# One tile shape for the loop of a recurrent attention kernel, and four stream buffers instead of six

## The chip, the core and the metric

The kernel runs on one core of a Trainium2 chip. The metric is the device time of one execution in microseconds (us). Three runs of the kernel before took 1918.54, 1930.37 and 1937.62 us; their median is 1930.37 us. One further execution was recorded by the profiler and took 1924.12 us; all rows below are from it.

## The reference

Two attentions over the same 2048 x 640 input are mixed by a gate. All tensors are bfloat16.

```
g = sigmoid((x * gate_w).sum(-1))            # one gate per row
out = g * A(x) + (1 - g) * B(x)

A: mem = mem0                                # 8 rows of 640
   for s in range(64):                       # segments of 32 rows
       h = concat(mem, x[32 s : 32 s + 32])  # 40 rows
       q, k, v = h Wq, h Wk, h Wv            # 32 heads of 192 columns each
       p = softmax(q k^T * 192**-0.5, masked) # query i sees key j where i < 8 or i >= j
       o = (p v) Wo                          # 6144 -> 640
       mem = o[:8];  out_A[s] = o[8:]

B: 32 heads of 20 columns, each row attends to 8 rows spaced 2 apart; then one product by wo
```

A is a recurrence: the first eight output rows of a segment are the memory of the next one, so the 64 segments run one after the other.

## The kernel before, in words

The work runs in stages: B with the gate (`part_b`), a prepass that makes the products of the last 8 rows of every segment (`prepass`), the loop over the 64 segments (`part_a`), and an end that makes the outputs of those last rows for all segments (`part_z`). In the loop h holds 32 rows: 8 of memory and the first 24 of the segment; queries, keys and values of the other 8 rows come from the prepass through a DRAM buffer (`zpk_dram`) by `load_z` and `load_vz` (L494 to L498).

**Weights.** Wq, Wk, Wv and Wo are cut in 80 slices of 128 x 1536 (384 KB). Most stay in SBUF (tiles `wres` and `wlate`). N_STREAM of them, 15 here, are loaded again in each segment into WBUFS buffers, 6 here (tile `wst`, `load_slice`, L369 to L378). `weights_setup` (L335 to L367) spreads the streamed ones evenly over a modelled order of use: 163 ns for a slice and a table of gaps. SP's queue issues all these loads in the order of use, and each waits until the matmuls of the slice that held its buffer are done.

**The loop.** Heads are worked on in four groups R of eight, in two halves h of two groups. Each projection is four matmuls side by side: 32 rows of h stand in 32 columns of the array (`tile_position=(0, 32 * j)`), and each of the four column tiles multiplies its own 384 columns of a slice.

- `m_qk(i, kcs)` (L511): queries (i even) or keys (i odd) of group R = i // 2, in PSUM; when the last slice is done ScalarE copies 128 x 384 to SBUF (L524).
- `t_qk(i)` (L527): three transposes of 128 x 128 (L533), then VectorE copies all of it at once into `QTa` (L536) or `KT` (L540).
- `s_a(R, chunks)` (L549) and `s_b(h, chunks)` (L561): the scores of the own keys and of the prepass keys `KTz`. A head's 192 columns are one chunk of 128 and half of another. FULL chunks (t = 0, 2) use tiles of 128 rows x 32 columns; chunk t = 1 holds the halves of two heads, and HALF works on it in tiles of 64 x 32, rows 0 to 63 for one head and 64 to 127 for the other.
- `e_exp` (L571): exponential on ScalarE (L573), masks on VectorE. `e_norm` (L581): row sums by two matmuls with a 128 x 128 block matrix `bones` (L587, L589), Ln and Exp on ScalarE (L592, L593), two products on VectorE (L594, L595). Its PSUM buffer comes from the pool `psx` of two, which the transposes share.
- `m_v` (L597) values, `pv_half` (L610) probabilities times values in tiles of 32 rows x 128 or 64 columns (L622, L626), `o_group` (L652) the output product (L659).
- `sel` (L664): picks the 8 memory rows out of the output product by matmuls with `sel_m` (L669) in 128 x 128 tiles, three for part "oa" and two for "ob"; VectorE copies them into the next h (L672).

The order of TensorE and ScalarE is written out by hand (L507, and L675 to L734); VectorE and GpSimd are ordered by the framework. In a segment it is, shortened:

```
m_qk(0, 0-2) m_qk(1, 0) sel(ob) m_qk(1, 1-2) tail m_qk(0, 3-4) m_qk(1, 3-4)
m_qk(2, 0-2) t0 t1 m_qk(2, 3-4) m_qk(3) s_a(0)
m_qk(4, 0-3) t2 t3 m_qk(4, 4) [store, load_vz issued by ScalarE] m_qk(5) s_a(1) s_b(0) e_exp(0)
m_qk(6, 0-3) t4 t5 m_qk(6, 4) m_qk(7) e_norm(0) s_a(2) m_v(0) t6 t7 m_v(1) s_a(3) s_b(1) e_exp(1)
m_v(2) pv_half(0) e_norm(1) m_v(3) oa(0-5) pv_half(1) ob(0-2) oa(6-11) ob(3-8) sel(oa) ob(9-11)
```

Here t0 stands for `t_qk(0)`, oa and ob for `o_group`. `KT` is the first 768 columns of the tile `KV`, whose columns are used again in the same segment for the values `V` and the transposed outputs; `KTz`, `QTa`, the probabilities and the copied output product share the tile `ZQ`.

Of the kernel before, what the change touches and what calls it, by code (L numbers as in the profile page):

```python
# [10 lines left out]
BF = mybir.dt.bfloat16  # L11
F32 = mybir.dt.float32
I32 = mybir.dt.int32

N_STREAM = 15
N_LATE = 55
N_LATE2 = 11
WBUFS = 6

_DEV = {"mode": "full"}  # L20

# [3 lines left out]
class _K:  # L25
# [309 lines left out]
    def weights_setup(self):  # L335
# [125 lines left out]
    def part_a(self):  # L461
        nc, tc, KC, S = self.nc, self.tc, self.KC, self.S
# [3 lines left out]
        with ctx:  # L466
            pers = ctx.enter_context(tc.tile_pool(name="a_pers", bufs=1))
# [3 lines left out]
            KTz = ZQ[:, 608:992].rearrange("p (r c) -> p r c", c=12)  # L471
            Vz = ZQ[:, 224:608]
            QTa = ZQ[:, 992:2144].rearrange("p (b r c i) -> p b r c i", b=6, r=2, i=8)
            Es = [ZQ[:, 608 * h:608 * h + 224].rearrange("p (a f) -> p a f", a=2) for h in range(2)]
            zst = ZQ[:, 32:416]
            oTz = zst.rearrange("p (c q) -> p c q", q=8)
            whi = ZQ[:, 1376:1376 + 640]
            KV = pers.tile([128, 1536], BF, name="KV")
            KT = KV[:, 0:768].rearrange("p (c k) -> p c k", k=32)
            V = [KV[:, f0:f0 + 384] for f0 in (0, 768, 384, 1152)]  # L480
# [12 lines left out]

            def load_z(s):  # L494
                nc.scalar.dma_start(ZQ[:, 608:1376], self.zpk_dram[s, :, 384:1152])

            def load_vz(s):
                nc.scalar.dma_start(Vz, self.zpk_dram[s, :, 0:384])  # L498
# [9 lines left out]
            for s in range(nseg):  # L508
                pqs, sts, pSs = {}, {}, {}

                def m_qk(i, kcs):  # L511
                    R, m = i // 2, ("q", "k")[i % 2]
                    if i not in pqs:
                        pqs[i] = psm.tile([128, 512], F32, tag="m", name="ps_qk")
                    pq = pqs[i]
                    for kc in kcs:
                        sl = self.get_slice((m, R, kc))
                        for j in range(4):
                            nc.tensor.matmul(pq[32 * j:32 * j + 32, 0:384], lhsT=hT[:, kc, :],  # L519
                                             rhs=sl[:, 384 * j:384 * j + 384], start=(kc == 0), stop=(kc == KC - 1),  # L520
                                             tile_position=(0, 32 * j), skip_group_check=True)
                    if kcs[-1] == KC - 1:
                        st = KV[:, 768 + 384 * (i % 2):1152 + 384 * (i % 2)]
                        nc.scalar.copy(st, pq[:, 0:384])  # L524
                        sts[i] = st

                def t_qk(i):  # L527
                    R = i // 2
                    st = sts.pop(i)
                    pT = psx.tile([128, 1024], BF, tag="x", name="ps_qkT")  # L530
                    pT = pT[:, 0:384].rearrange("p (t j b i) -> p t j b i", t=3, j=4, i=8)
                    for t in range(3):
                        nc.tensor.transpose(pT[:, t, :, :, :].rearrange("p j b i -> p (j b i)"),  # L533
                                            st[:, 128 * t:128 * t + 128], self.ident[:])
                    if i % 2 == 0:
                        nc.vector.tensor_copy(  # L536
                            q_blocks(R)[:, 1:5, :, :].rearrange("p b c i -> p c b i"),
                            pT.rearrange("p t j b i -> p (t j) b i"))
                    else:
                        nc.vector.tensor_copy(KV[:, 384 * (R % 2):384 * (R % 2) + 384],  # L540
                                              pT.rearrange("p t j b i -> p (t j b i)"))

                def q_blocks(R):
                    b0 = 1 - R // 2
                    return QTa[:, b0:b0 + 5, R % 2, :, :]

                FULL, HALF = ((0, 0, 0, 128), (2, 1, 0, 128)), ((1, 0, 0, 64), (1, 1, 64, 128))

                def s_a(R, chunks):  # L549
# [3 lines left out]
                    for t, par, k0, k1 in chunks:  # L553
                        for j in range(4):
                            c = 4 * t + j
                            nc.tensor.matmul(pSs[h][32 * j:32 * j + 32, par, 40 * r:40 * r + 40],  # L556
                                             lhsT=KT[k0:k1, 12 * r + c, :], rhs=q_blocks(R)[k0:k1, :, c, :],
                                             start=(r == 0 and t != 1), stop=False,
                                             tile_position=(k0, 32 * j), skip_group_check=True)

                def s_b(h, chunks):  # L561
                    for t, par, k0, k1 in chunks:
                        for j in range(4):
                            c = 4 * t + j
                            nc.tensor.matmul(  # L565
                                pSs[h][32 * j:32 * j + 32, par, 80:112],
                                lhsT=KTz[k0:k1, :, c],
                                rhs=QTa[k0:k1, 1 - h:3 - h, :, c, :].rearrange("p b r i -> p r b i"),
                                start=False, stop=(t == 1), tile_position=(k0, 32 * j), skip_group_check=True)

                def e_exp(h):  # L571
                    E = Es[h]
# [8 lines left out]
                def e_norm(h):  # L581
                    E = Es[h]
                    EA = E[:, :, 0:80].rearrange("p a (r q) -> p a r q", q=40)
                    EB = E[:, :, 80:112].rearrange("p a (r q) -> p a r q", q=16)
                    pz = psx.tile([128, 512], F32, tag="x", name="ps_Z")
                    pz = pz[:, 0:160].rearrange("p (a r q) -> p a r q", a=2, r=2)
                    nc.tensor.matmul(pz.rearrange("p a r q -> p a (r q)"), lhsT=self.bones[:], rhs=E[:, :, 0:80],  # L587
                                     start=True, stop=False, skip_group_check=True)
                    nc.tensor.matmul(pz[:, :, :, 0:16], lhsT=self.bones[:], rhs=EB, start=False, stop=True,  # L589
                                     skip_group_check=True)  # L590
                    rz = pz
                    nc.scalar.activation(rz, pz, ACT.Ln)  # L592
# [92 lines left out]
                m_qk(3, range(KC)); s_a(0, FULL); s_a(0, HALF)  # L685
# [5 lines left out]
                for chunks in (FULL, HALF):  # L691
                    s_a(1, chunks)
                    s_b(0, chunks)
                e_exp(0)
                m_qk(6, (0, 1, 2, 3)); t_qk(4); t_qk(5); m_qk(6, (4,))
                m_qk(7, range(KC)); e_norm(0); s_a(2, FULL); s_a(2, HALF)
                m_v(0); t_qk(6); t_qk(7)
                m_v(1)
                for chunks in (FULL, HALF):
                    s_a(3, chunks)  # L700
                    s_b(1, chunks)
# [26 lines left out]
                if s + 1 < nseg:  # L728
                    pm = psS.tile([128, 2, 512], F32, tag="S", name="ps_mem")
# [136 lines left out]
```

## Time and profile before

| what | value |
|---|---|
| three runs, median | 1930.37 us |
| profiled execution, its time | 1924.12 us |
| its span, first to last instruction | 1922.4 us |
| mean granted TensorE clock | 0.987 |
| B and gate, prepass | 0 to about 240 us, to about 455 us |
| loop, 64 segments | about 460 to 1865 us |
| one segment, mean of 62 | 22.0 us (20.7 to 24.1) |
| end (`part_z`) | about 1865 to 1922 us |
| PE busy in the window 1000 to 1200 us | 187.04 us |
| DMA share and rate in that window | 0.90, 296 GB/s |

A segment is measured from one copy of "ob" (L734) to the next. In the profile PE stands for matmuls, PEld for weight loads, DVE for VectorE, ACT for ScalarE, POOL for GpSimd and SP for SyncE; a form such as 128*32 is the array tile, rows by columns, that a matmul uses. A row of a timeline gives the start, the length from the first start to the last end, the engine, the line, the tiles written and read, the count, and in brackets the idle time before it with what ended it. "issue" means that the engine waited for nothing that the profile shows.

### The profile page before, as it was taken

What the parts mean: (1) busy time and instruction counts of PE and PEld (TensorE: products, weight loads), DVE (VectorE), ACT (ScalarE), POOL (GpSimd) and SP (SyncE); (2) the same over time, 40 slices, a digit from 0 to 9 for tenths busy, and PEclk for the clock granted to TensorE, in tenths of its full rate; (3) what the DMA queues carried; (4) which work ended last, traced back from release to release, by engine and by line L of the source; (5) the groups of instructions that cost most, each with busy time, mean ns of one, the idle gap of its engine ahead of it and who ended that gap; (6) DMA issues with size and microseconds to landing.
All of it is one profiled execution on the core that took longest, in us unless ns stands there. A gap on an engine that the chain in (4) does not pass through costs nothing.

```text
span 1922.4 us, 90977 instructions
## 1 busy us (share of the span) xinstructions
PE 1731.9 (90%) x41120; PEld 1034.7 (54%) x41135; DVE 743.9 (39%) x2047; ACT 838.2 (44%) x1865; POOL 41.0 (2%) x70
## 2 busy tenths in 40 slices
PE   3898997897998999999999999999999999999989
PEld 1455543344555555555555555555555555555557
DVE  1565588922333333333333333333333333333320
ACT  1766688922333333443334433334433433333340
POOL 3111000001000000000000000000000000000000
PEclk9999999998999999999999999999999999999989
DMA  9112189869988899999999988899899988998981
GB/s 277 33 43 46 42 242 286 112 165 301 301 288 294 273 297 286 298 303 300 299 294 304 295 295 293 283 297 304 292 302 297 300 295 289 296 305 291 300 285 28
DMA packets 340968, 486.86 MB, mean 253 GB/s; under 512 B 148964, under 2 KB 209892, under 8 KB 340580
## 3 DMA queue, kind: packets, MB, share of 16 engines
q1 hardware_dynamic: 198608, 419.28, 66.2%
q10 hardware_dynamic: 141972, 61.76, 13.9%
q8 instruction: 322, 5.28, 1.1%
q14 instruction: 66, 0.54, 0.1%
HBM read 446.61 MB, written 35.91 MB: 251 GB/s over the span
## 4 chain that ended last, share of the span: by engine, by line
PE 73%; DVE 7%; ACT 7%; DMA 6%; issue 5%; ACTq 1%; SPq 0%; DVEq 0%
PE ps_qk L519 24%; PE ps_v L602 12%; PE ps_wo L659 11%; PE ps_qkT L533 6%; DVE ZS L73 5%; PE ps_S L556 3%; PE ps_oT L622 3%; PE ps_z L799 3%; PE ps_bqk L219 2%; ACT bP L242 2%; PE ps_pre L422 2%; ACT KV L524 2%; DVE KV L632 1%; PE ps_S L565 1%; DMA zpk_dram<-ZS 1%
## 5 line engine op out<-in xcount | busy, mean ns | idle before, releaser
L524 ACT CAST KV<-ps_qk 128x384 bf16<-128x384 f32 x512 | 238.8, 479 | 414.2 <-PE ps_qk L519 358.9
L519 PEld LDWEIGHTS <-hT 128*32 128x32 bf16 x10240 | 237.7, 96 | 183.4 <-issue 64.5
L519 PE MATMUL ps_qk<-wlate_k,hT 128*32 128x384 bf16 x4352 | 247.9, 328 | 4.3 <-issue 4.3
L602 PE MATMUL ps_v<-wlate_v,hT 128*32 128x384 bf16 x4096 | 226.7, 329 | 5.2 <-issue 5.1
L659 PEld LDWEIGHTS <-KV 128*32 128x32 bf16 x6144 | 170.0, 96 | 101.1 <-DVE KV L632 27.3
L519 PE MATMUL ps_qk<-wres_q,hT 128*32 128x384 bf16 x2560 | 164.6, 331 | 28.9 <-ACT KV L524 20.9
L536 DVE COPY ZQ<-ps_qkT 128x384 bf16<-128x384 bf16 x256 | 91.2, 356 | 237.2 <-PE ps_qkT L533 237.1
L659 PE MATMUL ps_wo<-wlate_oa,KV 128*32 128x384 bf16 x2304 | 154.1, 330 | 11.6 <-issue 3.9
L519 PE MATMUL ps_qk<-wst,hT 128*32 128x384 bf16 x1792 | 153.8, 330 | 1.9 <-issue 1.5
L602 PEld LDWEIGHTS <-hT 128*32 128x32 bf16 x5120 | 114.1, 96 | 73.0 <-issue 15.1
L632 DVE CAST KV<-ps_oT 128x192 bf16<-128x192 f32 x256 | 79.9, 353 | 170.7 <-ACT KV L632 170.7
L659 PE MATMUL ps_wo<-wlate_ob,KV 128*32 128x256 bf16 x2688 | 133.5, 278 | 12.2 <-issue 11.9
L533 PE MATMUL ps_qkT<-ident,KV 128*128 128x128 bf16 x1536 | 141.6, 221 | 2.1 <-ACT KV L606 0.3
L533 PEld LDWEIGHTS <-KV 128*128 128x128 bf16 x1536 | 87.9, 98 | 93.8 <-issue 92.6
L71 ACT CAST ZS<-ps_pre 128x512 bf16<-128x512 f32 x48 | 123.9, 3051 | 13.3 <-DMA zpk_dram<-ZS 6.4
L73 DVE CAST ZS<-ps_pre 128x512 bf16<-128x512 f32 x48 | 123.3, 2963 | 11.9 <-DMA zpk_dram<-ZS 7.7
L659 PE MATMUL ps_wo<-wst,KV 128*32 128x384 bf16 (+1 forms) x1152 | 115.3, 312 | 3.6 <-issue 2.7
L632 ACT CAST KV<-ps_oT 128x192 bf16<-128x192 f32 x256 | 69.7, 325 | 108.5 <-PE ps_oT L626 105.8
L519 PE MATMUL ps_qk<-wlate_q,hT 128*32 128x384 bf16 x1536 | 108.3, 330 | 0.0
L672 DVE CAST hT<-ps_mem 128x24 bf16<-128x24 f32 x126 | 22.5, 179 | 214.1 <-PE ps_mem L669 214.1
L556 PE MATMUL ps_S<-ZQ,KV 128*32 128x40 bf16 (+1 forms) x4096 | 102.7, 186 | 0.7 <-DMA ZQ<-zpk_dram 0.4
L556 PEld LDWEIGHTS <-KV 128*32 128x32 bf16 (+1 forms) x4096 | 78.0, 93 | 37.4 <-issue 1.8
(128 smaller groups left out, 2304.8 us busy)
## 6 DMA issues: line engine op xcount, KB each, us to landing
wst<-in_A_Wq_dram SPq DMA_DIRECT2D x260, 384.0 KB
wst<-in_A_Wv_dram SPq DMA_DIRECT2D x260, 384.0 KB
wst<-wscr SPq DMA_DIRECT2D x256, 384.0 KB
wst<-in_A_Wk_dram SPq DMA_DIRECT2D x195, 384.0 KB
zpk_dram<-ZS ACTq DMA_DIRECT2D x8, 1536.0 KB
ZQ<-zpk_dram ACTq DMA_DIRECT2D x64, 192.0 KB
wlate_k<-in_A_Wk_dram SPq DMA_DIRECT2D x17, 384.0 KB
wlate_v<-in_A_Wv_dram SPq DMA_DIRECT2D x16, 384.0 KB
```

The costliest lines, as they stand in the source:

```text
L71: nc.scalar.copy(out, in_)
L73: nc.vector.tensor_copy(out, in_)
L519: nc.tensor.matmul(pq[32 * j:32 * j + 32, 0:384], lhsT=hT[:, kc, :], rhs=sl[:, 384 * j:384 * j + 384], start=(kc == 0), stop=(kc == KC - 1 ...
L524: nc.scalar.copy(st, pq[:, 0:384])
L533: nc.tensor.transpose(pT[:, t, :, :, :].rearrange("p j b i -> p (j b i)"), st[:, 128 * t:128 * t + 128], self.ident[:])
L536: nc.vector.tensor_copy(q_blocks(R)[:, 1:5, :, :].rearrange("p b c i -> p c b i"), pT.rearrange("p t j b i -> p (t j) b i"))
L556: nc.tensor.matmul(pSs[h][32 * j:32 * j + 32, par, 40 * r:40 * r + 40], lhsT=KT[k0:k1, 12 * r + c, :], rhs=q_blocks(R)[k0:k1, :, c, :], st ...
L602: nc.tensor.matmul(pv[32 * j:32 * j + 32, 0:384], lhsT=hT[:, kc, :], rhs=sl[:, 384 * j:384 * j + 384], start=(kc == 0), stop=(kc == KC - 1 ...
L622: nc.tensor.matmul(out[:, r, t, :], lhsT=V[2 * h + r][ks, f0:f1], rhs=E[ks, par, 40 * r:40 * r + 40], start=(r == 0 and t == 0), stop=Fals ...
L632: cp(oTxs[2 * h + j // 2][:, 6 * (j % 2):6 * (j % 2) + 6, :], pos[j // 2][:, j % 2, 0:240].rearrange("p (c q) -> p c q", q=40)[:, :, 8:40])
L659: nc.tensor.matmul(pso[part][32 * jj:32 * jj + 32, 0:n], lhsT=oTxs[2 * (R // 2) + j // 2][:, 6 * (j % 2) + 3 * (R % 2) + t, :], rhs=o_weig ...
L799: nc.tensor.matmul(ps[32 * q:32 * q + 32, 0:nf], lhsT=oz[n, q][:, 24 * (R // 2) + 6 * j + 3 * (R % 2) + t, :], rhs=wo[part, c // nc_][:, c ...
```

## The change

The loop's products are brought to one tile shape, 128 rows x 32 columns; only `pv_half` keeps its own. A transpose becomes four, one for each 32 columns of its source; each of the two row-sum matmuls becomes four; each selection matmul becomes four. For the scores, chunk t = 1 is no longer worked on in 64-row tiles: the key half of the other head is zero instead. `KT` keeps rows 0 to 63 of that chunk with zeros below (written by GpSimd in each segment), and a new tile `KP` holds rows 64 to 127 with zeros above, for own keys (`KTp`) and prepass keys (`KTzp`). VectorE's copy of the transposed keys becomes three copies, and `load_z` is followed by a copy and a memset on GpSimd. `s_a` and `s_b` do all four chunks in one call. One weight slice fewer is streamed, and the stream has four buffers instead of six. The pools of PSUM and the order of the calls stay.

```diff
-N_STREAM = 15
+N_STREAM = 14
-WBUFS = 6
+WBUFS = 4
...
+            KP = pers.tile([128, 384], BF, name="KP")
+            nc.gpsimd.memset(KP[0:64, :], 0.0)
+            KTp = [KP[:, 128 * r:128 * r + 128].rearrange("p (j k) -> p j k", k=32) for r in range(2)]
+            KTzp = KP[:, 256:384].rearrange("p (r j) -> p r j", j=4)
...
             def load_z(s):
                 nc.scalar.dma_start(ZQ[:, 608:1376], self.zpk_dram[s, :, 384:1152])
+                nc.gpsimd.tensor_copy(KTzp[64:128], KTz[64:128, :, 4:8])
+                nc.gpsimd.memset(KTz[64:128, :, 4:8], 0.0)
...
-                        nc.tensor.transpose(pT[:, t, :, :, :].rearrange("p j b i -> p (j b i)"),
-                                            st[:, 128 * t:128 * t + 128], self.ident[:])
+                        for f in range(4):
+                            fs = slice(32 * f, 32 * f + 32)
+                            nc.tensor.transpose(pT[fs, t, :, :, :].rearrange("p j b i -> p (j b i)"),
+                                                st[:, 128 * t + 32 * f:128 * t + 32 * f + 32], self.ident[:],
+                                                tile_position=(0, 32 * f))
...
-                        nc.vector.tensor_copy(KV[:, 384 * (R % 2):384 * (R % 2) + 384],
-                                              pT.rearrange("p t j b i -> p (t j b i)"))
+                        kt = KV[:, 384 * (R % 2):384 * (R % 2) + 384].rearrange("p (t f) -> p t f", t=3)
+                        kp = pT.rearrange("p t j b i -> p t (j b i)")
+                        nc.vector.tensor_copy(kt[:, 0:3:2, :], kp[:, 0:3:2, :])
+                        nc.vector.tensor_copy(kt[0:64, 1, :], kp[0:64, 1, :])
+                        if R < 2:
+                            nc.gpsimd.memset(kt[64:128, 1, :], 0.0)
+                        nc.vector.tensor_copy(KTp[R % 2][64:128].rearrange("p j k -> p (j k)"), kp[64:128, 1, :])
...
-                FULL, HALF = ((0, 0, 0, 128), (2, 1, 0, 128)), ((1, 0, 0, 64), (1, 1, 64, 128))
+                CHUNKS = ((0, 0), (2, 1), (1, 0), (1, 1))
...
-                                             lhsT=KT[k0:k1, 12 * r + c, :], rhs=q_blocks(R)[k0:k1, :, c, :],
-                                             start=(r == 0 and t != 1), stop=False,
-                                             tile_position=(k0, 32 * j), skip_group_check=True)
+                                             lhsT=KTp[r][:, j, :] if (t, par) == (1, 1) else KT[:, 12 * r + c, :],
+                                             rhs=q_blocks(R)[:, :, c, :], start=(r == 0 and t != 1), stop=False,
+                                             tile_position=(0, 32 * j), skip_group_check=True)
...
-                    nc.tensor.matmul(pz.rearrange("p a r q -> p a (r q)"), lhsT=self.bones[:], rhs=E[:, :, 0:80],
-                                     start=True, stop=False, skip_group_check=True)
-                    nc.tensor.matmul(pz[:, :, :, 0:16], lhsT=self.bones[:], rhs=EB, start=False, stop=True,
-                                     skip_group_check=True)
+                    for z in range(2):
+                        for j in range(4):
+                            js = slice(32 * j, 32 * j + 32)
+                            out, rhs = (pz[js, :, :, 0:16], EB) if z else (
+                                pz[js].rearrange("p a r q -> p a (r q)"), E[:, :, 0:80])
+                            nc.tensor.matmul(out, lhsT=self.bones[:, js], rhs=rhs, start=(z == 0), stop=(z == 1),
+                                             tile_position=(0, 32 * j), skip_group_check=True)
...
-                        nc.tensor.matmul(pm[:, p, 8 * (m - m0):8 * (m - m0) + 8], lhsT=whi[:, m * 128:(m + 1) * 128],
-                                         rhs=self.sel_m[:], start=(m == m0), stop=(m == m1 - 1),
-                                         skip_group_check=True)
+                        for f in range(4):
+                            nc.tensor.matmul(pm[32 * f:32 * f + 32, p, 8 * (m - m0):8 * (m - m0) + 8],
+                                             lhsT=whi[:, m * 128 + 32 * f:m * 128 + 32 * f + 32], rhs=self.sel_m[:],
+                                             start=(m == m0), stop=(m == m1 - 1), tile_position=(0, 32 * f),
+                                             skip_group_check=True)
```

More of the change, by code (lines that the diff above doesn't have):

```diff
@@ L545, in q_blocks, with s_a @@
                     return QTa[:, b0:b0 + 5, R % 2, :, :]
-                FULL, HALF = ((0, 0, 0, 128), (2, 1, 0, 128)), ((1, 0, 0, 64), (1, 1, 64, 128))
-                def s_a(R, chunks):
+                CHUNKS = ((0, 0), (2, 1), (1, 0), (1, 1))
+                def s_a(R):
                     h, r = R // 2, R % 2
@@ L552, in s_a @@
                         pSs[h] = psS.tile([128, 2, 512], F32, tag="S", name="ps_S")
-                    for t, par, k0, k1 in chunks:
+                    for t, par in CHUNKS:
                         for j in range(4):
@@ L556, in s_a, with s_b @@
                             nc.tensor.matmul(pSs[h][32 * j:32 * j + 32, par, 40 * r:40 * r + 40],
-                                             lhsT=KT[k0:k1, 12 * r + c, :], rhs=q_blocks(R)[k0:k1, :, c, :],
-                                             start=(r == 0 and t != 1), stop=False,
-                                             tile_position=(k0, 32 * j), skip_group_check=True)
-                def s_b(h, chunks):
-                    for t, par, k0, k1 in chunks:
+                                             lhsT=KTp[r][:, j, :] if (t, par) == (1, 1) else KT[:, 12 * r + c, :],
+                                             rhs=q_blocks(R)[:, :, c, :], start=(r == 0 and t != 1), stop=False,
+                                             tile_position=(0, 32 * j), skip_group_check=True)
+                def s_b(h):
+                    for t, par in CHUNKS:
                         for j in range(4):
@@ L566, in s_b @@
                                 pSs[h][32 * j:32 * j + 32, par, 80:112],
-                                lhsT=KTz[k0:k1, :, c],
-                                rhs=QTa[k0:k1, 1 - h:3 - h, :, c, :].rearrange("p b r i -> p r b i"),
-                                start=False, stop=(t == 1), tile_position=(k0, 32 * j), skip_group_check=True)
+                                lhsT=KTzp[:, :, j] if (t, par) == (1, 1) else KTz[:, :, c],
+                                rhs=QTa[:, 1 - h:3 - h, :, c, :].rearrange("p b r i -> p r b i"),
+                                start=False, stop=(t == 1), tile_position=(0, 32 * j), skip_group_check=True)
                 def e_exp(h):
@@ L684, in part_a @@
                 m_qk(2, (0, 1, 2)); t_qk(0); t_qk(1); m_qk(2, (3, 4))
-                m_qk(3, range(KC)); s_a(0, FULL); s_a(0, HALF)
+                m_qk(3, range(KC)); s_a(0)
                 m_qk(4, (0, 1, 2, 3)); t_qk(2); t_qk(3); m_qk(4, (4,))
@@ L690, in part_a @@
                 m_qk(5, range(KC))
-                for chunks in (FULL, HALF):
-                    s_a(1, chunks)
-                    s_b(0, chunks)
+                s_a(1)
+                s_b(0)
                 e_exp(0)
                 m_qk(6, (0, 1, 2, 3)); t_qk(4); t_qk(5); m_qk(6, (4,))
-                m_qk(7, range(KC)); e_norm(0); s_a(2, FULL); s_a(2, HALF)
+                m_qk(7, range(KC)); e_norm(0); s_a(2)
                 m_v(0); t_qk(6); t_qk(7)
                 m_v(1)
-                for chunks in (FULL, HALF):
-                    s_a(3, chunks)
-                    s_b(1, chunks)
+                s_a(3)
+                s_b(1)
                 e_exp(1)
```

## The prediction, as put on record before the result

> **What bounds the kernel now.** I read the page first, then a timeline of one segment on PE and ACT, then the waits of the steady loop (600 to 1800 us, 55 segments), then the DMA queues of that window. The page:
>
> ```profile
> PE 1731.9 (90%) x41120; PEld 1034.7 (54%) x41135; DVE 743.9 (39%) x2047; ACT 838.2 (44%) x1865; POOL 41.0 (2%) x70
> ...
> q8 instruction: 322, 5.28, 1.1%
> ...
> PE 73%; DVE 7%; ACT 7%; DMA 6%; issue 5%; ACTq 1%; SPq 0%; DVEq 0%
> ```
>
> TensorE's order of work is the chain, and busy 90% hides what is lost inside it. The timeline of PE shows the loss:
>
> ```profile
> 1003.89 0.67 PE L519 MATMUL ps_qk<-wres_q,hT 128*32 128x384 bf16 x12 [0.25 <-ACT KV L524]
> 1004.49 0.51 PE L533 MATMUL ps_qkT<-ident,KV 128*128 128x128 bf16 x6
> 1004.93 0.35 PE L519 MATMUL ps_qk<-wres_q,hT 128*32 128x384 bf16 x4
> 1005.11 0.34 PE L519 MATMUL ps_qk<-wst,hT 128*32 128x384 bf16 x4
> 1005.27 0.99 PE L519 MATMUL ps_qk<-wlate_k,hT 128*32 128x384 bf16 x20
> 1006.08 0.36 PE L556 MATMUL ps_S<-ZQ,KV 128*32 128x40 bf16 x16
> 1006.37 0.35 PE L519 MATMUL ps_qk<-wst,hT 128*32 128x384 bf16 x4
> ```
>
> Four projection matmuls side by side start every 0.163 us (1005.11 to 1005.27). The third group of the first row starts at 1004.22, so the transposes could start at 1004.38; they start at 1004.49. Six of them start 0.057 apart ((0.51 - 0.22) / 5), so the next group could start at 1004.83; it starts at 1004.93. Each change of tile shape costs about 0.10 us, and a segment has 29.
>
> The second loss is irregular. In the waits of PE, "issue" names no engine and no transfer, yet lasts up to 1.8 us; one such hole, in the timeline:
>
> ```profile
> PE ps_wo L659 <- issue: 16.9, 20, 1.8
> PE ps_qk L519 <- ACT KV L524: 14.1, 55, 0.3
> PE ps_oT L622 <- issue: 9.8, 13, 1.5
> PE ps_oT L626 <- issue: 9.2, 10, 1.4
> ```
> ```profile
> 1039.83 0.18 PE L626 MATMUL ps_oT<-ZQ 32*64 32x32 bf16 x2
> 1040.84 0.21 PE L626 MATMUL ps_oT<-ZQ 32*64 32x32 bf16 x6 [0.82 <-issue]
> ```
>
> Queue q8 explains it. Its 322 packets carry 5.28 MB, 16.4 KB each; PE and PEld have 82,255 instructions, 64 B each, 255 to a packet: q8 brings TensorE its own instructions in blocks of 256. The packet records around the hole: one runs from 1038.40 to 1039.54, and PE resumes 1.30 us after it. Over the loop, 74 holes of over 0.5 us lie 255.3 instructions (or a multiple) apart, and each ends 1.2 to 1.7 us (mean 1.41) after a q8 packet. After a hole the next packet starts 1.1 to 4.0 us (mean 2.23) later and takes 1.02: one block ahead, no more. A refill takes 2.23 + 1.02 + 1.41 = 4.66 us beside the stream, and a segment's 565 matmuls and as many weight loads are 4.41 blocks in 22.0 us. The mean hole by the block's own time (hole left out), from the starts in the records: 0.93 us for blocks under 3.5 us (29 of them), 0.61 for 3.5 to 4, 0.35 for 4 to 4.5, 0.13 for 4.5 to 5, 0.04 to 5.5, none above. That is 0.27 a block, 1.2 us a segment; a segment's own time is 20.8.
>
> SP's queue is not behind: a slice lands 3.84 us after its issue (median of the packet records; 4.5 at the 95th percentile, 5.3 at most), and no PE row above waits for one.
>
> **What the change saves on TensorE, per segment.** It removes 23 of the 29 changes of shape (the 6 of pv_half stay).
> - Transposes: four pairs, 0.11 before and 0.10 after each: 0.84. The 24 quarter transposes of a pair go four at a time, like the projections, at the old 0.057 a group: no more.
> - Scores: 16 matmuls took 0.29 with their two changes (1006.08 to 1006.37). Four groups of four take 0.03 each, since eight start within 0.06 in the next call: 0.12, saving 0.17, twice. The 32 of s_a and s_b go from 0.48 to 0.30 (prepass keys, read with a stride, 0.045 a group): 0.175, twice. Together 0.69.
> - Sums: 0.19 around e_norm(0), 0.10 in e_norm(1). Selections: 0.10 and 0.07 for each part: 0.34.
>
> Gross 2.16 us. Some of it only uncovers another engine:
> - t7 waits for the PSUM buffer of e_norm(0). From the last group of m_qk(7) the chain is fixed: ACT's copy, Ln, Exp, DVE's products, 2.03 us (1011.07 to 1013.10). TensorE would come 1.36 after. It already waits 0.2; all saved in between is lost: sums 0.19, s_a(2) 0.17, one entry 0.10: 0.46.
> - t5 needs ACT's copy of keys, queued behind two DMA issues:
>
> ```profile
> 1008.03 0.48 ACT L524 CAST KV<-ps_qk 128x384 bf16<-128x384 f32 x1 [1.19 <-PE ps_qk L519]
> 1008.11 0.58 ACTq L752 DMA_DIRECT2D out_dram<-a  x1
> 1008.73 0.48 ACTq L498 DMA_DIRECT2D ZQ<-zpk_dram  x1
> 1009.31 0.48 ACT L524 CAST KV<-ps_qk 128x384 bf16<-128x384 f32 x1 [0.80 <-PE ps_S L565]
> ```
> The copy is ready 2.27 after the group m_qk(4, 4) starts; TensorE comes at 2.10 (5 + 4 groups 1.47, scores 0.30, t4 0.17, one step 0.16): 0.17 lost.
> - sel(oa) comes when ACT's copy L727 is done, as 45 waits of it already show: entry 0.10 lost. The first m_qk(0, 3-4) waits for DVE's L672: 0.03.
>
> Lost 0.76, net 1.40 us (between 1.2, if pv_half(1) stays on DVE's L594, and 2.16, if nothing is uncovered). The segment's own time falls from 20.8 to 19.4.
>
> **What it adds.** DVE: one key copy (351 ns) becomes three. By the rows 128x384 (351), 128x24 (183) and 128x16 (175) they end about 0.24 us later. The last is ready 0.94 us after the last transpose; five to seven groups (0.82 to 1.14) and three score groups (0.09) stand before its reader. Cost 0; without that cover at most 0.24 a group R. POOL: three memsets and a copy per segment, by 32-row rows 0.18 to 0.26 us each, bounded by 128x640 at 0.82. They stand behind load_z's landing, some 4 us after an issue that precedes sel(oa) by 2; s_a(0) comes 5 us after it: 0, or up to 1 us if a landing takes 6. The own load of one more resident slice at the start: 1.3 us (384 KB at 296 GB/s), taken as 1.
>
> Buffers: a slice now must land within four uses less its own, 4 x 19.4/14 - 0.6 = 4.9 us, against 3.84 (six: 6 x 22.0/15 - 0.6 = 8.2). Mostly covered: 0; the other end is 0.5 us on two slices a segment, 1 us. One slice of 15 less lowers the load of the DMA engines by 6% a segment.
>
> TensorE's instructions: transposes 24 to 96, sums 4 to 16, selections 5 to 20: 99 matmuls and 99 weight loads more, 664 pairs, 5.19 blocks in 19.4 us: 3.74 us of own time a block instead of 4.7. By the table above, a hole of 0.65 a block (0.61 at 3.75, and a little for the spread to both sides), 3.4 us a segment instead of 1.2. Bounds: 0.27 as now; 1.0 if each hole leaves the next block without the lead that it has now (refill 4.66 against 3.74, spread included). I take 0.65, which has rows of this very loop.
>
> **The sum.** 19.4 + 3.4 = 22.8 us against 22.0: +0.8, times 64 = 51 us, and 1 at the start. From the profiled 1924 us: 1976. (The median of runs is 1930, 0.3% above that execution.)
>
> [...]
>
> [...]
>
> **The rivals.**
> - Refills stay covered: faster. Place: the block boundaries; price: 0.27 a block as now, 19.4 + 1.4 = 20.8, 64 x -1.2 gives 1847. It decides below (22.0 - 19.4) / 5.19 = 0.50 us a block. For it: six per cent less stream, and q8 shares its engines with the stream. Against it: the 58 blocks under 4 us, with 0.77 on average.
> - Refills bind fully: 1.0 a block, 19.4 + 5.2 = 24.6, 1924 + 64 x 2.6 = 2090. For it: two holes in a row happen already; against it: a slower segment also thins the stream, and with it the 2.23 us of queueing.
> - Four buffers are too few: refills as now, but 1 us a segment of landing on top of the forecast: 2040. Against it: 1 us of slack at the median.
> - The changes of shape don't go away, since the stall is the operand's and not the shape's: net 0, refills at 20.8 / 5.19 = 4.0 us, 0.48 a block: 1924 + 64 x 1.3 = 2007. Against it: the same 0.10 at every change, and none between L556 and L565.
>
> **How the numbers follow.** Forecast (0.45 to 0.85 us a block, 1905 to 2040, its own likely stretch 1930 to 2010): 0.52, of which 0.10 lies within 1%. Refills covered (1800 to 1905): 0.24, of which 0.02 within 1%. Refills bind fully: 0.14; late landings: 0.05; shape stalls stay: 0.05. A measurement can tell about 1% (19 us) from no change. Faster 0.22, same 0.12, slower 0.66. The range 1860 to 2090 leaves out the lower end of the covered case and what lies above full binding.
>
> **What would show it.** Right: some 372 q8 packets (50 more); holes at every second boundary or more, 3 us a segment; no step at L533, L587, L669 beyond 0.163; t7 still 2.0 us behind m_qk(7). Wrong: "issue" no larger than now, or PE waiting for wst, POOL or the third key copy.

## The result

Four runs after: 2017.72 to 2034.44 us, median 2026.68; four before: median 1927.06. The ratio is 1.0505 [1.0466, 1.0545]: about 5% slower. The profiled execution took 2028.84 us (span 2027.0, mean granted clock 0.970). Line numbers move in the kernel after: ACT's key and query copy is L530, the transposes L541, `s_a` L570, `s_b` L579, the sums L606, `m_v` L619, `pv_half` L639 and L643, `o_group` L676, the selections L687.

From the page of the kernel after, the lines of busy time, of the queue q8, and of the chain that ended last:

```profile
PE 1680.0 (83%) x47456; PEld 1099.0 (54%) x47456; DVE 821.5 (41%) x2559; ACT 841.1 (41%) x1865; POOL 94.5 (5%) x327
...
q8 instruction: 371, 6.08, 1.2%
...
PE 58%; issue 12%; DVE 10%; ACT 9%; DMA 9%; ACTq 1%; SPq 0%; DVEq 0%; POOL 0%
```

PE has 6,300 matmuls more and is busy 52 us less, yet the span is longer: PE's share of the chain fell from 73% to 58%, "issue" rose from 5% to 12%. q8 has 49 packets more. The mean over the whole loop, before and then after (columns: window, its length, busy time and count of PE, PEld, DVE, ACT, POOL, then the granted clock, the DMA share, GB/s):

```profile
474.00:1860.00 1386.00, 1290.20 (x35481) 787.69 (x35477) 464.18 (x1698) 540.77 (x1507) 0.00 (x0) 1.00 0.91 296
```
```profile
478.00:1966.00 1488.00, 1230.96 (x41696) 848.47 (x41683) 541.11 (x2203) 543.50 (x1507) 51.49 (x248) 0.98 0.84 260
```

PE is busy 59 us less and the window is 102 us longer. The mean segment went from 21.99 to 23.63 us (62 of them); ahead of the loop there are 4 us more, and the end takes the same (57.1 and 56.5). The DMA share fell with the pace of the loop; nothing here says that the stream holds it back. PE's timeline after, at the place that the prediction showed of before (start, length, idle time before in brackets):

```profile
1045.35 0.67 PE L525 MATMUL ps_qk<-wres_q,hT 128*32 128x384 bf16 x12 [0.26 <-ACT KV L530]
1045.84 0.52 PE L541 MATMUL ps_qkT<-ident,KV 128*32 128x128 bf16 x24
1046.17 0.51 PE L525 MATMUL ps_qk<-wres_q,hT 128*32 128x384 bf16 x8
1046.49 0.35 PE L525 MATMUL ps_qk<-wst,hT 128*32 128x384 bf16 x4
1046.66 0.51 PE L525 MATMUL ps_qk<-wlate_k,hT 128*32 128x384 bf16 x6
1048.43 0.67 PE L525 MATMUL ps_qk<-wlate_k,hT 128*32 128x384 bf16 x10 [1.27 <-issue]
```

The transposes follow the third group by 0.16 us (1045.84 - 1045.35 - 2 x 0.163), and the next projection starts 0.33 us after them, six groups at 0.056: the steps at the changes of shape are gone. Then, in the middle of `m_qk(3)`, PE stands still for 1.27 us for nothing that the profile names; a q8 packet had run from 1046.16 to 1047.10, and PE resumes 1.33 us after its end. The waits of PE after (600 to 1900 us: what waited for what, us in total, times, longest):

```profile
PE ps_qk L525 <- issue: 33.5, 38, 1.9
PE ps_v L619 <- issue: 27.5, 26, 2.1
PE ps_qkT L541 <- issue: 26.7, 26, 2.0
PE ps_oT L639 <- issue: 21.7, 20, 2.1
PE ps_S L570 <- issue: 18.0, 22, 2.6
PE ps_qkT L541 <- DVE ZQ L612: 16.6, 32, 0.6
PE ps_qk L525 <- ACT KV L530: 13.6, 53, 0.3
PE ps_oT L639 <- DVE KV L625: 10.5, 29, 0.4
...
PE ps_qk L525 <- DMA wst<-in_A_Wk_dram: 1.7, 4, 0.6
PE ps_qk L525 <- DMA wst<-in_A_Wq_dram: 1.4, 3, 0.9
```

Holes now sit in every stage, the projections first. Counted as in the prediction (over 0.5 us, ended by an instruction that comes 1.1 to 1.75 us after a q8 packet), there are 186 of them against 76, 3.43 us a segment against 1.22. They keep to a place in the stream of instructions: counted with the sequencer's own, every 256th. Of the 197 gaps between starts over 0.3 us that end 1.2 to 1.6 us after a q8 packet, 190 fall on the same eight of the 256 places (before: 85 of 96). The waits for `wst` are short. Two rows are new: t7 behind DVE's L612, and `pv_half` behind L625, VectorE's copy of values.

### The profile page after: what moved, and what is told of

Same layout as the page of the kernel before. It is cut to its first block, busy times and chain, and to the rows that moved or that the text cites. A ratio compares the mean times of both kernels' runs of the same rounds, so it can differ in the third digit from the quotient of the medians.

```text
span 2027.0 us, 104719 instructions
## 1 busy us (share of the span) xinstructions
PE 1680.0 (83%) x47456; PEld 1099.0 (54%) x47456; DVE 821.5 (41%) x2559; ACT 841.1 (41%) x1865; POOL 94.5 (5%) x327
## 4 chain that ended last, share of the span: by engine, by line
PE 58%; issue 12%; DVE 10%; ACT 9%; DMA 9%; ACTq 1%; SPq 0%; DVEq 0%; POOL 0%
PE ps_qk L525 19%; PE ps_wo L676 8%; PE ps_v L619 8%; DVE ZS L73 5%; PE ps_qkT L541 4%; DMA wst<-in_A_Wq_dram 3%; PE ps_oT L639 3%; PE ps_z L816 3%; PE ps_pre L422 2%; ACT bP L242 2%; PE ps_bqk L219 2%; DVE KV L649 2%; PE ps_S L570 2%; ACT KV L649 2%; DMA wst<-in_A_Wk_dram 1%
## 5 line engine op out<-in xcount | busy, mean ns | idle before, releaser
L530 ACT CAST KV<-ps_qk 128x384 bf16<-128x384 f32 x512 | 239.0, 479 | 438.5 <-PE ps_qk L525 390.0
L525 PEld LDWEIGHTS <-hT 128*32 128x32 bf16 x10240 | 268.2, 96 | 208.2 <-issue 107.6
L525 PE MATMUL ps_qk<-wlate_k,hT 128*32 128x384 bf16 x4096 | 261.4, 329 | 21.2 <-issue 20.3
L619 PE MATMUL ps_v<-wlate_v,hT 128*32 128x384 bf16 x4096 | 255.8, 335 | 26.9 <-issue 26.9
L676 PEld LDWEIGHTS <-KV 128*32 128x32 bf16 x6144 | 179.5, 99 | 103.5 <-DVE KV L649 32.6
L541 PE MATMUL ps_qkT<-ident,KV 128*32 128x128 bf16 x6144 | 156.8, 221 | 49.8 <-issue 30.5
L525 PE MATMUL ps_qk<-wres_q,hT 128*32 128x384 bf16 x2816 | 177.1, 330 | 24.3 <-ACT KV L530 19.2
L619 PEld LDWEIGHTS <-hT 128*32 128x32 bf16 x5120 | 139.2, 98 | 80.4 <-issue 48.1
L541 PEld LDWEIGHTS <-KV 128*32 128x32 bf16 x6144 | 128.7, 98 | 82.7 <-issue 37.8
L676 PE MATMUL ps_wo<-wlate_oa,KV 128*32 128x384 bf16 x2560 | 157.8, 346 | 6.1 <-issue 4.5
L676 PE MATMUL ps_wo<-wlate_ob,KV 128*32 128x256 bf16 x2688 | 136.5, 284 | 3.6 <-issue 3.5
L525 PE MATMUL ps_qk<-wlate_q,hT 128*32 128x384 bf16 x1536 | 126.2, 328 | 7.5 <-issue 7.5
L676 PE MATMUL ps_wo<-wst,KV 128*32 128x384 bf16 (+1 forms) x896 | 105.2, 320 | 12.0 <-issue 2.2
L619 PE MATMUL ps_v<-wst,hT 128*32 128x384 bf16 x1024 | 100.4, 334 | 7.3 <-issue 7.2
L639 PE MATMUL ps_oT<-ZQ,KV 32*128 32x40 bf16 (+1 forms) x4096 | 77.0, 186 | 35.3 <-issue 21.7
L587 ACT ACTIVATE ZQ<-ps_S 128x224 bf16<-128x224 f32 x128 | 46.0, 360 | 132.7 <-PE ps_S L579 128.3
```

The source lines that it names most:

```text
L541: nc.tensor.transpose(pT[fs, t, :, :, :].rearrange("p j b i -> p (j b i)"), st[:, 128 * t + 32 * f:128 * t + 32 * f + 32], self.ident[:], ...
L587: nc.scalar.activation(E, pSs[h][:, :, 0:112], ACT.Exp, scale=scale_a)
L619: nc.tensor.matmul(pv[32 * j:32 * j + 32, 0:384], lhsT=hT[:, kc, :], rhs=sl[:, 384 * j:384 * j + 384], start=(kc == 0), stop=(kc == KC - 1 ...
L639: nc.tensor.matmul(out[:, r, t, :], lhsT=V[2 * h + r][ks, f0:f1], rhs=E[ks, par, 40 * r:40 * r + 40], start=(r == 0 and t == 0), stop=Fals ...
L676: nc.tensor.matmul(pso[part][32 * jj:32 * jj + 32, 0:n], lhsT=oTxs[2 * (R // 2) + j // 2][:, 6 * (j % 2) + 3 * (R % 2) + t, :], rhs=o_weig ...
```

## The experiments

The theory: TensorE's instructions come in blocks that are refilled one ahead, and more and shorter instructions leave the refill uncovered. The rivals: the thinner stream (late slices), the added VectorE and GpSimd work, or the 32-column loads themselves.

| kernel | median us | before, same chip | ratio [95%] | segment | holes | rest |
|---|---|---|---|---|---|---|
| b_stream | 1929.81 | 1932.31 | 0.9995 [0.9971, 1.0019] | 22.16 | 1.30 | 20.86 |
| b_trans | 2008.84 | 1932.31 | 1.0416 [1.0372, 1.0460] | 23.40 | 3.13 | 20.27 |
| b_splitv | 2056.45 | 1932.31 | 1.0661 [1.0610, 1.0712] | 24.23 | 2.53 | 21.70 |
| b_scores | 1928.31 | 1932.31 | 0.9987 [0.9959, 1.0015] | 22.18 | 1.53 | 20.65 |
| b_nostream | 1841.86 | 1932.52 | 0.9517 [0.9485, 0.9549] | 20.81 | 0.28 | 20.52 |
| a_nostream | 1828.31 | 1932.52 | 0.9442 [0.9406, 0.9478] | 20.58 | 0.86 | 19.71 |
| a_t128 | 1947.87 | 1932.52 | 1.0080 [1.0051, 1.0110] | 22.31 | 1.59 | 20.72 |
| b_scores5 | 1928.06 | 1932.52 | 0.9980 [0.9955, 1.0004] | 22.09 | 1.74 | 20.36 |
| s5_norm | 1916.26 | 1930.14 | 0.9909 [0.9876, 0.9941] | 21.75 | 1.55 | 20.20 |
| b_norm | 1923.43 | 1930.14 | 0.9968 [0.9942, 0.9995] | 22.01 | 1.38 | 20.63 |

Segment, holes and rest are us per segment from each profile; here holes count from 0.3 us, and the rest, the segment's own time, is the segment without them. On this scale before has 21.99 = 1.30 + 20.69 and after 23.63 = 3.58 + 20.04.

### b_stream: only the buffers and the streamed slices

Before, with
```diff
-N_STREAM = 15
+N_STREAM = 14
-WBUFS = 6
+WBUFS = 4
```


> The kernel before with only the stream's part of the change (14 streamed slices, four buffers). Theory (TensorE waits for the refills of its instruction blocks; 99 more matmuls and weight loads a segment made it slower): the 565 matmuls of a segment stay, so 4.41 blocks and holes of about 1.2 us a segment stay or shrink a little with 6% less stream; 1910 to 1932 us. Rival (four buffers let slices land late): most of the 100 us of the change, 1970 to 2030 us, with waits of PE for wst.

The same time, the same holes. From its waits of PE (600 to 1800 us):

```profile
PE ps_oT L622 <- issue: 13.1, 18, 1.8
...
PE ps_v L602 <- DMA wst<-in_A_Wv_dram: 1.4, 2, 1.1
```

In the whole loop 8 waits for a slice take 3.5 us. Four buffers instead of six and one slice less together change nothing that can be told; the run does not tell the two apart.

### b_trans: only the transposes

Before, with the transposes of the change:
```diff
-                        nc.tensor.transpose(pT[:, t, :, :, :].rearrange("p j b i -> p (j b i)"),
-                                            st[:, 128 * t:128 * t + 128], self.ident[:])
+                        for f in range(4):
+                            fs = slice(32 * f, 32 * f + 32)
+                            nc.tensor.transpose(pT[fs, t, :, :, :].rearrange("p j b i -> p (j b i)"),
+                                                st[:, 128 * t + 32 * f:128 * t + 32 * f + 32], self.ident[:],
+                                                tile_position=(0, 32 * f))
```


> The kernel before with only the transposes in four 32-column pieces, stream as before (15 slices, six buffers). Theory: 637 matmuls a segment, 4.98 blocks; the eight changes of shape go (0.84 us), own time a block about 4.0 us, holes about 0.45 a block, 2.2 us a segment instead of 1.2: about 22.3 us a segment, 1950 us (1925 to 1985). Rival (buffers or key copies made the change slow): the drains' 0.84 us come through, 1870 to 1890 us.

The direction was right and the size too small: 4.2% slower, most of the whole loss, with no added copy, GpSimd work or buffer change. Its waits of PE (600 to 1800 us):

```profile
PE ps_qk L519 <- issue: 28.2, 31, 2.3
PE ps_oT L625 <- issue: 24.1, 24, 2.2
PE ps_v L605 <- issue: 18.6, 20, 2.1
```

Few of the holes are at the transposes: they lie in the projections and `pv_half`, wherever a block ends. The segment's 72 pairs more (a pair is a load and its matmul) add 1.83 us of holes; own time fell by only 0.42. Part of the missing gain may be the clock: 54 us of the loop ran at half of it (see the last section), by accounting up to 0.35 us a segment.

### b_splitv: more instructions, same shape, same columns

Before, each `m_v` matmul of 384 columns as two of 192:
```diff
-                        for j in range(4):
-                            nc.tensor.matmul(pv[32 * j:32 * j + 32, 0:384], lhsT=hT[:, kc, :],
-                                             rhs=sl[:, 384 * j:384 * j + 384], start=(kc == 0), stop=(kc == KC - 1),
-                                             tile_position=(0, 32 * j), skip_group_check=True)
+                        for c0 in (0, 192):
+                            for j in range(4):
+                                nc.tensor.matmul(pv[32 * j:32 * j + 32, c0:c0 + 192], lhsT=hT[:, kc, :],
+                                                 rhs=sl[:, 384 * j + c0:384 * j + c0 + 192],
+                                                 start=(kc == 0), stop=(kc == KC - 1),
+                                                 tile_position=(0, 32 * j), skip_group_check=True)
```


> The kernel before with each value matmul of 384 columns split in two of 192: 80 more matmuls and weight loads a segment, 645 in all, the same columns streamed, no tile shape changed, no other engine touched. Theory: 5.04 blocks of 4.1 us own time, holes 0.4 to 0.53 a block, 2.0 to 2.7 us a segment instead of 1.2: 1980 to 2025 us. Rivals (buffers, key copies, GpSimd, tile shapes): 1927 to 1935 us, since twenty more steps cost 2.5 ns each or so.

6.6% slower: the direction that only the refill theory gives, and more than it gave. The edit touches no transpose, score, sum, selection or buffer; it adds 80 pairs a segment. Splitting is not dear in itself. I timed a segment by phases, from the first matmul of one stage to that of the next, and took the 10th percentile of each, that is segments where no hole fell in that phase. The phases then add up to 20.56 us against 20.53 before, and the medians of the `m_v(0)` and `m_v(1)` phases are unchanged (+0.01, +0.05). In the mean the loss sits further on, from `m_v(2)` to `pv_half(1)` (+0.64, +0.44, +1.31), where a block passes fastest: 55 blocks of the loop have an own time under 3 us, with 1.8 us of hole behind each on average; before there are 3. The mean own time of a block is 4.24 us, longer than in the kernel after (3.78), so it is these short blocks and not the mean that make the holes. Its waits (600 to 1800 us), then one hole in its timeline:

```profile
PE ps_v L603 <- issue: 43.0, 30, 2.8
PE ps_oT L624 <- issue: 25.0, 21, 2.5
PE ps_oT L628 <- issue: 18.7, 13, 2.3
```
```profile
1017.57 0.35 PE L603 MATMUL ps_v<-wst,hT 128*32 128x192 bf16 x8
1017.74 0.33 PE L603 MATMUL ps_v<-wlate_v,hT 128*32 128x192 bf16 x6
1020.08 0.76 PE L603 MATMUL ps_v<-wlate_v,hT 128*32 128x192 bf16 x26 [2.01 <-issue]
```

A q8 packet runs from 1017.67 to 1018.60, PE resumes 1.48 us after its end: it stops for 2 us in the middle of a slice's eight matmuls, with nothing that they wait for. Holes explain 1.23 us of the 2.24 that a segment grew. The other 1.0 is the rest; the loop ran 136 us at half clock against 12 before, and half of the difference over 62 segments is 1.0. So the clock can account for it; no run shows that it does.

### b_scores: the change without transposes, sums and selections

After, with these three put back (the first shown, the other two in the same manner):
```diff
-                        for f in range(4):
-                            fs = slice(32 * f, 32 * f + 32)
-                            nc.tensor.transpose(pT[fs, t, :, :, :].rearrange("p j b i -> p (j b i)"),
...
+                        nc.tensor.transpose(pT[:, t, :, :, :].rearrange("p j b i -> p (j b i)"),
+                                            st[:, 128 * t:128 * t + 128], self.ident[:])
...
```


> The change with transposes, row sums and selections put back as before: only the scores in 128-row tiles with zero-padded keys, three key copies, the GpSimd work, 14 slices and four buffers. Theory: still 565 matmuls a segment; eight changes of shape less, 0.6 to 0.7 us of own time gone, of which about half comes back as holes: 1885 to 1915 us, faster than before. Rival (key copies on VectorE, GpSimd or buffers cost the time): 1960 us or more.

Missed: no gain. But no loss either, though it keeps the three key copies, the GpSimd work, the zero-padded tiles and four buffers: none of them carries the 5%. Where the saving went, by its waits of PE (600 to 1800 us):

```profile
PE ps_qkT L539 <- DVE ZQ L606: 11.3, 50, 0.2
...
PE ps_v L613 <- DMA wst<-in_A_Wv_dram: 2.7, 6, 1.0
```

The first is t7 behind the sums' products, which the prediction named for the change. Slices cost 12.6 us in 21 waits over the loop, and the 10th percentile of the rest (19.86 us a segment, 20.20 before) shows more of the saving than its mean: holes rose by 0.23 and 36.6 us ran at half clock.

### b_nostream and a_nostream: refills with an idle queue

Each kernel with its loop fed from resident slices of the same matrix:
```diff
+        if getattr(self, "resident_only", False):
+            return self.res_tiles[next(k for k in self.res_tiles if k[0] == key[0])]
...
+        self.resident_only = True
```


> The kernel before, but in the loop a streamed slice is replaced by a resident one of the same matrix, so that no weights are loaded there (the values computed are others; the work of every engine is the same). Theory: with the DMA queues nearly empty a refill takes about 3.4 us instead of 4.6 and is covered by the 4.7 us of a block; holes go, 20.6 us a segment instead of 22.0: about 1840 us (1825 to 1865). Rival (key copies, GpSimd, tile shapes): says nothing of this kernel alone; the pair with the next one decides.

> The changed kernel, no weights loaded in the loop, as in b_nostream (the values computed are others; the work of every engine is the same). Theory: refills of 3.4 us against 3.65 us of own time a block leave small holes, about 1 us a segment; the removed changes of shape show: 19.9 us a segment, about 1795 us (1760 to 1830), faster than b_nostream by 1 to 4%. Rival (what the change adds on VectorE, GpSimd or in the array costs the time): as much slower than b_nostream as the change was, 3 to 5%, 1895 us or more.

The first landed on its number, 1841.86. The second lies at the upper end of its stretch, 1828.31, and missed its distance from the first: faster by 0.7% (the intervals of the two against before do not meet), where 1 to 4% was expected. The sign of the change flips all the same: with the stream after is 5% slower, without it slightly faster. The same 200 us (1000 to 1200) of b_nostream, then of a_nostream:

```profile
1000.00:1200.00 200.00, 195.62 (x5463) 121.11 (x5451) 70.64 (x260) 82.96 (x232) 0.00 (x0) 1.00 0.11 29
```
```profile
1000.00:1200.00 200.00, 184.46 (x6488) 127.51 (x6492) 84.28 (x344) 83.86 (x234) 7.45 (x36) 1.00 0.11 29
```

With DMA at 0.11 the next refill starts 1.0 us (median) after a block boundary in a_nostream, instead of 1.8 in the kernel after; before it is 2.0. (A boundary is every 256th instruction, from the place of the holes.) Holes nearly vanish in b_nostream (0.28 us a segment) and stay small in a_nostream (0.86), which runs the same 371 packets as after. So the large holes come where both meet: many short instructions, and queues loaded by the stream. Why a_nostream gains no more, by its waits of PE (600 to 1800 us):

```profile
PE ps_oT L642 <- DVE KV L628: 14.9, 40, 0.4
PE ps_qk L528 <- ACT KV L533: 14.4, 56, 0.3
PE ps_qkT L544 <- DVE ZQ L615: 13.2, 44, 0.5
PE ps_oT L642 <- issue: 6.2, 8, 1.0
```

In b_nostream ACT's row has 14.4 too, the last row 1.3, the wait for the sums' products 1.5 (once), and that for VectorE's copy of values is absent. The faster matmuls now wait for VectorE at two places, in most segments. At the 10th percentile the rest is 18.90 us; its mean is 19.71.

### a_t128: after, with whole transposes

```diff
-                        for f in range(4):
-                            fs = slice(32 * f, 32 * f + 32)
...
+                        nc.tensor.transpose(pT[:, t, :, :, :].rearrange("p j b i -> p (j b i)"),
+                                            st[:, 128 * t:128 * t + 128], self.ident[:])
```


> The changed kernel with the transposes put back to 128x128 (scores, sums, selections, 14 slices and four buffers as changed). Theory: 592 matmuls a segment, 4.63 blocks, own time 19.7 us, 4.25 a block, holes 0.4 a block, 1.9 us a segment, some half-clock stretches: 21.7 to 22.2 us, 1905 to 1945 us. Rival (the rest of the change costs as much as the transposes): 1970 us or more.

0.8% slower than before, just above the stretch. Taking 72 pairs a segment out of the kernel after gives back about 4 of the 5%, as putting them into the kernel before cost 4. What is left of the change costs the 0.8%.

### b_scores5: the scores with the old stream

b_scores, with
```diff
-N_STREAM = 14
+N_STREAM = 15
-WBUFS = 4
+WBUFS = 5
```


> As b_scores, but 15 streamed slices and five buffers, which takes the same memory. Theory: b_scores saved 0.55 us of own time a segment and lost it to the wait of the last transpose pair (0.2), landings (0.2) and holes; a fifth buffer takes the landings away: 1905 to 1925 us. Rival (landings were no cost, the rest of the stream matters): 1928 us as b_scores.

Missed: no wait for a slice is left, and the rest fell by 0.29 us, but the holes grew by 0.21 and the time stayed. What the landings had cost came back mostly as holes.

### s5_norm and b_norm: the sums later, so that t6 and t7 go first

b_scores5, and before (with its own score calls), each with
```diff
-                m_qk(7, range(KC)); e_norm(0); s_a(2)
+                m_qk(7, range(KC)); s_a(2)
...
                 m_v(1)
+                e_norm(0)
```


> b_scores5 with e_norm(0) moved behind m_v(1), so that the last transpose pair no longer waits for its PSUM buffer. Theory: of the 1.65 us from the last transposes to s_a(3) about 0.45 go; own time 20.4 to 19.95 us, about half of it comes back as holes, since blocks get shorter: 1905 to 1920 us, the fastest of all with streaming. Rival (that wait was covered by holes anyway): 1928 us as b_scores5.

> The kernel before with e_norm(0) moved in the same way and nothing else changed. Theory: only the 0.2 us that the last transposes wait there goes, and half of it comes back: 1920 to 1930 us, within 1% of before, so that the gain of s5_norm, if any, belongs to the scores and the move together. Rival (the move itself is worth as much as in s5_norm): 1905 to 1918 us.

Both hit. s5_norm is 0.9% faster than before, the fastest version with the stream (1916.26, where the kernel after took 2026.68; the kernel before took 1930.14 and 1927.06 beside them). The wait of t7 for L606 (10.8 us in 48 waits in b_scores5) has left its list:

```profile
PE ps_oT L633 <- issue: 18.1, 24, 1.5
PE ps_wo L670 <- issue: 17.1, 20, 1.7
PE ps_qk L525 <- ACT KV L530: 14.3, 56, 0.3
PE ps_v L613 <- issue: 9.4, 12, 1.6
```

What is left is ACT's copy, as before, and refills. Against before, the rest of s5_norm is 0.49 us a segment shorter (20.69 to 20.20) with the same number of q8 packets (322), and the holes are 0.25 larger (1.30 to 1.55): half of the saving comes back, as the blocks get shorter. (The profiled execution of s5_norm is its fastest, 1907.41.) In b_norm only the order changes: it gains 0.3%.

## Why the prediction was right, and where it was off

The sign and the mechanism were right, and the forecast's range (1905 to 2040) holds the result. Its size did not come out as well: the profiled time, 2028.84, is 53 us above the 1976 and above the forecast's likely stretch (1930 to 2010). The loss is 105 us where 52 were forecast, twice as much.

- **Shape steps.** Predicted gross 2.16 us a segment; the phases at their 10th percentile add up to 18.42 us against 20.53: 2.11. The rival that shape stalls stay falls.
- **Uncovered waits, 0.76.** t7 does wait for the sums' PSUM buffer (about 0.36 us a segment, 0.46 predicted); it starts 2.21 us (median) after the last group of `m_qk(7)`, 2.07 before. The 0.17 at t5 did not come: it starts 0.174 us after t4 (median), which is t4's own three groups. Without the clock and the two waits below, own time fell by 20.69 - 20.04 + 0.47 + 0.25 + 0.13 = 1.50, predicted 1.40.
- **Holes.** Predicted 372 packets, 0.65 us a block, 3.4 us a segment; measured 371, 0.67, 3.43. The prediction's table by the block's own time held in the kernel after. With a boundary at every 256th instruction the mean hole is 1.35 us behind blocks under 3 us (36 of them), 1.04 to 3.5 (93), 0.58 to 4 (63), 0.39 to 4.5 (88), 0.18 to 5 (28), and none above (13). The covered rival needed less than 0.50; full binding needed 1.0.
- **Its rivals' remark on queueing held.** After a hole the next refill starts 1.79 us later (2.21 before, by the same count), with the stream at 260 GB/s instead of 296; the blocks got shorter by more.
- **The term that was mis-sized is the own time, 19.4 us.** By the prediction's count of holes it measured 23.63 - 3.43 = 20.2, 0.8 above; times 64 that is 51 of the missing 53 us; the rest lies ahead of the loop, where 4 us came and 1 was forecast. The sum had no term for three things that together are as large. Granted clock: 61.4 us of the 62 segments at half clock against 3.4, by accounting at most 0.47 us a segment. The late copy of V[3], 0.25. Late slices, 17 waits, 7.9 us, 0.13, taken as 0.
- **The copy of V[3]** is an order on VectorE that the prediction did not look at. Before, then after, on VectorE's timeline:

```profile
1017.67 0.56 DVE L608 CAST KV<-ps_v 128x384 bf16<-128x384 f32 x1
1018.15 0.31 DVE L594 TENSOR_TENSOR ZQ<-ZQ,ps_Z 128x160 bf16<-128x160 bf16 x1
```
```profile
1038.12 0.32 DVE L611 TENSOR_TENSOR ZQ<-ZQ,ps_Z 128x160 bf16<-128x160 bf16 x1 [0.39 <-ACT ps_Z L610]
1038.35 0.21 DVE L612 TENSOR_TENSOR ZQ<-ZQ,ps_Z 128x64 bf16<-128x64 bf16 x1
1038.49 0.55 DVE L625 CAST KV<-ps_v 128x384 bf16<-128x384 f32 x1
```

Before, the copy of values goes ahead of the two products; after, behind them, and so in all 62 segments of each (VectorE's order is the framework's, not the hand's). `pv_half(1)` needs all three, and waits for the last: 36 gaps in the 62 segments, 15.6 us from start to start without the usual step. That the prediction took `pv_half(1)` to stay or not stay on L594 alone was too narrow.
- **Added VectorE and GpSimd work, taken as 0.** b_scores keeps it all and is not slower. Late slices: 0.13 us of the 1 us that the rival gave.
- **Summed.** The loop grew by 101 us: holes +141 (2.28 x 62), half clock up to +29, V copy and slices +23, own time saved up to -93.

Of 320 boundaries in the loop 60% have a hole. The rival of the 32-column loads falls as well: the six quarter-transpose groups above start 0.056 apart, where the prediction took 0.057, and in b_trans the loss is holes.

**What stays open.** The half clock's price is accounting, not an experiment: no run kept the long holes and took the half clock away. In a_nostream, whose "issue" waits last at most 1.0 us (600 to 1800 us), no stretch at half clock falls in the 62 segments. Why b_scores5's gain on landings came back as holes almost whole is open too, and so is what a_nostream would take without its two waits for VectorE, which no run took away.

## What to carry to other kernels

In this loop TensorE had a second limit beside its work: 256 instructions in some 4.7 us (4.66 by the packet records of before) while the DMA queues moved 296 GB/s. Without the stream (29 GB/s in a_nostream) a refill started 1.0 us after a boundary instead of 1.8. Before cutting an operation in four to avoid a stall, count the instructions per block and the block's own time, and look for "issue" gaps that end a fixed time after an instruction-queue packet (1.2 to 1.7 us after one of q8 in the kernel before). Look at the shortest blocks, not at the mean. The part of the gain that needs no more instructions (the zero-padded scores, with the sums moved behind the work that needs their buffer) was worth 0.9%; the whole, with 99 more pairs a segment, cost 5%.

## What was not expected of the hardware

**Half clock after short holes.** In the kernel after the granted clock drops to 0.5 in 18 stretches of the loop, in all 64.8 us; in b_splitv in 37, 136 us; before, 12 us; without the stream 6.8. One stretch of the kernel after, on PE's timeline, begins 1.4 us after a hole:

```profile
1222.99 0.20 PE L639 MATMUL ps_oT<-ZQ,KV 32*128 32x40 bf16 x3
1224.93 0.24 PE L639 MATMUL ps_oT<-ZQ,KV 32*128 32x40 bf16 x11 [1.75 <-issue]
```

Windows ahead of it, in it and behind it (columns as above; the clock is third from the end):

```profile
1223.25:1226.25 3.00, 1.32 (x73) 1.05 (x76) 0.26 (x1) 1.02 (x3) 0.00 (x0) 1.00 0.88 259
1226.50:1233.00 6.50, 6.00 (x126) 3.37 (x123) 1.98 (x8) 1.53 (x7) 0.07 (x1) 0.50 0.68 182
1233.25:1236.25 3.00, 2.82 (x89) 1.66 (x79) 0.74 (x3) 0.91 (x4) 0.63 (x3) 1.00 0.79 245
```

In windows of 0.25 us the drop lies at 1226.29 and the return at 1233.11, 6.83 us. The last gap over 0.5 us ahead of the drop lasted 1.75 us, amid small `pv_half` matmuls. Nor is it alone: of the 17 drops in the 62 segments 16 come within 2.3 us of the end of a gap of 0.5 to 2.6 us, and the other 16 stretches last 3.41 us each, half of this one's 6.83. What decides on a drop no run shows.

**The refill is one block ahead, and part of its wait goes with the stream.** TensorE behaves as if one block of 256 instructions were fetched ahead and no more: behind the 74 holes over 0.5 us of before, no packet starts sooner than 1.1 us after the hole (2.23 on average). The packet itself takes about as long at a low DMA load as beside the stream: in before 1.10 us on average from 60 to 240 us (DMA share 0.18) and 1.02 in the loop (0.91). The time from a boundary until it starts went from 1.8 us (after) to 1.0 (a_nostream, the same instructions without the stream). These 0.8 us are about what the change took from a block's own time, 4.64 us on average before and 3.78 after.
